# The low part of the squares moves from GpSimd to the Vector engine, with new due times

## The chip, the cores and the metric

The kernel runs on one core of one Trainium2 chip. The metric is the device time of one launch in microseconds (us). Three runs of the kernel before took 1542.89, 1548.58 and 1553.07 us; the median is 1548.58 us.

## The reference

Three layers follow one another on 3072 tokens (4 batches of 768 steps, 8 heads of 40 channels):

```python
for t in range(S):                       # attention with a 40x40 state per batch and head
    y[t] = r[t] @ state
    Sa = state @ a[t]
    state = state * w[t] - outer(Sa, b[t]) + outer(v[t], k[t])
h = x @ w_in                             # first feed-forward: 320 -> 2048 -> 320
g = relu(h) ** 2
x = g @ w_out
p = domain_probs / domain_probs.sum(-1)  # second: 4 experts, 320 -> 1024 -> 320
out = sum(p[:, e] * (relu(x @ w1[e]) @ w2[e]) for e in range(4))
```

All inputs are float32. Where the kernel needs more than one float32r product gives, it splits a number into a rounded high part and a low part (the number minus its high part), and multiplies both.

## The kernel before, in words

**Attention.** The 768 time steps are cut into 12 chunks of 64, and each chunk into two steps by batch pair, so that there are 24 steps s = 0 to 23. Two steps make one block k = 0 to 11. A step loads its inputs (`ld_in`, `ld_r`, `ld_v`, `ld_rf`, `ld_xv`, and the decay factors `ld_wd`), makes running products of the decay with a scan on the Vector engine (DVE; tile `P`, line 379, which reads tile `wd`) and reciprocals of them (line 399), scales k, b and a with them on GpSimd (lines 403 and 411), multiplies them on TensorE (PE), masks results on DVE (lines 493 and 609) and adds the state (lines 624 and 625).

**The inverse.** Each block solves a small triangular system: `invert` reads a matrix `mu` back from DRAM (line 682), runs 31 pairs of DVE instructions on it (line 699 writes `tmp`, line 702 updates `t`, each pair needing the one before), turns the result on ScalarE (ACT, line 709), writes it to DRAM (line 714) and reads it back in another layout (line 723) into `t11` and `TT`. DVE then transposes it (line 564) and PE goes on (line 570). There is one buffer each for `mu` and `t`, so block k + 1 loads `mu` after block k has been written out.

**First feed-forward.** `moe1` takes a block's 256 tokens. SP, the queue that issues the transfers, gathers them with 12 small transfers (line 815); ACT rounds them to `xh` (line 826) and DVE makes the low part `xl` (line 829). Then 16 units follow, one for each 128 hidden channels. A unit has eight products into `h` (line 208, called l1), relu on ACT (`r`, line 761), the square rounded to float32r on ACT (`gh`, line 764), the square in float32 in place (`r`, line 766), the low part `gl = r - gh` (line 769), and six products into `py` (lines 213, 214 and 217, called l2; only line 217 needs `gl`). Its weights come as 48 raw pieces that are decoded during the first blocks.

**Second feed-forward.** After block 10 the attention is over. Block 11 of the first feed-forward and all of the second (lines 971 and on) run in a fixed order with PE as the bound.

**The order of the work.** All engines run their queues in order. For attention, inverse, first feed-forward (blocks 0 to 10) and weight decoding, a planner (class `Schedule`) decides the order once, when the program is built: every operation has an engine, dependences, an assumed duration and a due time, and each engine takes the operation that can start first, and among those the one due first. Due times are a block's start (`DUE["block"]` apart) minus a lead from the table `LEAD`. `PORT` lists operations of DVE and GpSimd that the planner does not let overlap.

Of the kernel before, what the change touches and what calls it, by code (L numbers as in the profile page):

```python
# [7 lines left out]
F32 = mybir.dt.float32  # L8
# [3 lines left out]
ALU = mybir.AluOpType  # L12
# [30 lines left out]
def sub(base, dims):  # L43
# [2 lines left out]

DUE = dict(block=58.06, step=[-2.17, 3.5, -6.04, 5.05, -21.7], invert=[18.92, -23.0, -54.58], ffn=-0.1, w=[-71.6, 2.35])
LEAD = dict(  # L50
    ld_wd=131.3, ld_in=120.8, scan=117.1, m=121.4, t_load=121.1, t=88.2, t_out=173.3, ld_r=73.9, ld_xv=79.2,
    vm=77.6, f=72.9, kbt=67.6, x=65.1, merge=59.0, tx=76.4, ys=65.8, yq=54.5, x1=54.5, split=46.7,
)


class Schedule:
# [11 lines left out]
    STAY = 2.0  # L68

    PORT = dict(  # L70
        DVE=("P", "t", "x1l", "w_clamp", "w_shift", "w_sign", "w_pow", "w_mul"),
        POOL=("sq", "scale_a", "kb", "yq", "yf"),
    )

    def __init__(self):
# [2 lines left out]
    def op(self, name, eng, fn, due, deps=(), dur=0.47, alloc=(), prev=None, lat=None):  # L78
        assert name not in self.ops, name
        lat = (2.1 if eng == "SP" else 0.13) if lat is None else lat  # L80
        self.ops[name] = (eng, fn, due, list(deps) + [prev], dur, alloc, prev, lat)
# [66 lines left out]
def tile_delta_rule_moe(  # L148
# [15 lines left out]
    pe, act, dve, pool, sp = nc.tensor, nc.scalar, nc.vector, nc.gpsimd, nc.sync  # L164
# [55 lines left out]
    op = sch.op  # L220
# [451 lines left out]
    mdd, x1 = {}, {}  # L672
# [84 lines left out]
    def moe1_sq(k, f, i):  # L757
        g = gg[k, f]
        if i == 0:
            g["r"] = fp.tile([128, 256], F32, tag="g0", name=f"r{k}_{f}")  # L760
            act.activation(g["r"], g["ps"], AF.Relu)  # L761
        elif i == 1:
            g["gh"] = fp.tile([128, 256], F32R, tag="gh", name=f"gh{k}_{f}", bufs=3)
            act.activation(g["gh"], g["r"], AF.Square)  # L764
        elif i == 2:
            act.activation(g["r"], g["r"], AF.Square)  # L766
        else:
            g["gl"] = fp.tile([128, 256], F32R, tag="gl", name=f"gl{k}_{f}", bufs=3)
            pool.tensor_tensor(g["gl"], g["r"], g["gh"].bitcast(F32), ALU.subtract)  # L769

    def moe1_l2(k, f):
        if f == 0:
# [15 lines left out]
    def y1_out(k):  # L788
        sp.dma_start(y1d[k], yy[k])
# [15 lines left out]
    def moe1(k, tt):  # L805
        v = {}
        nw = [("w_low", 3 * NF1 - 1)]

        def to_x1(i):
            if i == 0:  # L810
                v["raw"] = buf3(f"xr{k}", "ws", 5).rearrange("p (c x) -> p c x", c=3)
            y = st[2 * k]["y"]
            r0, kc, hd, e0, e1 = MOVES[i]
            src = y[64 * (hd % 2) + e0:64 * (hd % 2) + e1, hd // 2].rearrange("q a x -> q (a x)")
            sp.dma_start(v["raw"][r0:r0 + e1 - e0, kc], src)  # L815

        xt = ("xh", "xl")

        def xbuf(i):
            return ("ws", 5) if k % 2 else (xt[i], 1)  # L820

        def split(i):
            t = buf3(f"{xt[i]}{k}", *xbuf(i))
            t = t.bitcast(F32R).rearrange("p (c x) -> p c x", c=3)
            if i == 0:
                act.copy(t, v["raw"])  # L826
                v["xh"] = t
            else:
                dve.tensor_tensor(t, v["raw"], v["xh"].bitcast(F32), ALU.subtract)  # L829
                x1[k] = (v["xh"], t, v["raw"])  # L830
                if dbg is not None:
                    sp.dma_start(dbg[k], v["raw"])

        ys = [("yq", 2 * k + b, h) for b in range(2) for h in range(2)]
        done = [("x1h", k), ("x1l", k)]
        for i in range(len(MOVES)):
            op(("tx1", k, i), "SP", lambda i=i: to_x1(i), tt - LEAD["x1"], ys + ([] if i else [("x1l", k - 1)]), 0.65, prev=("tx1", k, 0) if i else None,
               alloc=[] if i else [("ws", 5, done)])
        moved = [("tx1", k, i) for i in range(len(MOVES))]
        end = [("l1", k, NF1 - 1)]  # L840
        op(("x1h", k), "ACT", lambda: split(0), tt - LEAD["split"], moved, 0.73, alloc=[xbuf(0) + (end,)])
        op(("x1l", k), "DVE", lambda: split(1), tt - LEAD["split"], [("x1h", k)], 0.87, alloc=[xbuf(1) + (end,)])
        for f in range(NF1):
            t0 = tt + PB * f / NF1
            i = NF1 * k + f
            if i >= units:
                break
            u = lambda d: divmod(i + d, NF1)
            op(("l1", k, f), "PE", lambda f=f: moe1_l1(k, f), t0 - 3,
               [("x1l", k), ("l1",) + u(-1), ("w_low", 3 * f + 2), ("w_low", 3 * f)], 0.9,  # L850
               alloc=[("l1", 2, [("sq", k, f, 0)]), ("g0", 2, [("sq", k, f, 2), ("sq", k, f, 3)])])
            dep = {0: [("l1", k, f)], 3: [("sq", k, f, 2)]}
            al = [None, ("gh", 3, [("l2", k, f)]), None, ("gl", 3, [("l2", k, f)])]
            for j in range(4):
                op(("sq", k, f, j), "POOL" if j == 3 else "ACT", lambda f=f, j=j: moe1_sq(k, f, j), t0 - 2,
                   dep.get(j, [("sq", k, f, j - 1)]) + [("sq",) + u(-1) + (j,)], (0.28, 0.31, 0.31, 0.69)[j],
                   alloc=[al[j]] if al[j] else [])
            op(("l2", k, f), "PE", lambda f=f: moe1_l2(k, f), t0 + 3,
               [("sq", k, f, 3), ("l2",) + u(-1), ("w_low", 3 * f + 1)], 0.85,
               alloc=[("l2", 1, [("y1", k, 0), ("y1", k, 1)])] if f == 0 else [])  # L860
        if NF1 * (k + 1) <= units:
            for t in range(2):
                op(("y1", k, t), "ACT", lambda t=t: y1_copy(k, t), tt + PB - 2, [("l2", k, NF1 - 1)] + ([("y1", k, 0)] if t else []), 0.34,
                   alloc=[] if t else [("ws", 5, [("y1o", k)])])
            op(("y1d", k), "POOL", lambda: y1_double(k), tt + PB + 3, [("y1", k, 0), ("y1", k, 1)], 0.3)
            op(("y1o", k), "SP", lambda: y1_out(k), tt + PB + 4, [("y1d", k)], 0.47)


    nblk = nsteps // 2
    PB, F0 = DUE["block"], 80.0  # L870
    units = NF1 * (nblk - 1)
    for s in range(nsteps):
        attention(s, F0 + PB / 2 * s + DUE["step"][min(s, len(DUE["step"]) - 1)])
    for k in range(nblk):
        invert(k, F0 + PB * k + DUE["invert"][min(k, len(DUE["invert"]) - 1)])
        moe1(k, F0 + PB * k + DUE["ffn"])
    for n in range(3 * NF1):
        weights(n, F0 + DUE["w"][0] + DUE["w"][1] * n)
    sch.run()
    actx.close()  # L880
    items = [divmod(i, NF1) for i in range(units, NF1 * nblk)]
    ffn = []
# [75 lines left out]
    for e, k, f in items:  # L958
# [9 lines left out]
        gh = fp.tile([128, 256], F32R, tag="gh", name=f"zh{e}_{k}_{f}", bufs=3)  # L968
        gl = fp.tile([128, 256], F32R, tag="gl", name=f"zl{e}_{k}_{f}", bufs=3)
# [103 lines left out]
```

## Time and profile before

| | |
|---|---|
| runs | 1542.89, 1548.58, 1553.07 us |
| the profiled execution's own time | 1543.77 us |
| its span, first to last instruction | 1541.9 us |
| mean granted clock of TensorE | 0.977 of full speed |
| busy in the span: PE, DVE, ACT, GpSimd | 1424.5, 810.1, 732.8, 344.7 us |
| 192 instructions of line 769 (`gl`) on GpSimd | 143.9 us, 752 ns each |

The span has three parts: a start until the first block's tokens are split (to 118.9 us), the stretch in which attention and first feed-forward are interleaved (to 799.1 us), and the rest, in which PE hardly pauses. In the rows "idle" is time in which an engine's next instruction waited, with the instruction that released it. POOL is GpSimd in the rows, SPq the queue of transfers, PEclk the granted clock of TensorE.

### The profile page before, as it was taken

How to read it: one execution, taken by the hardware profiler on the slowest of the kernel's cores; microseconds unless marked ns; L12 is line 12 of the kernel's file. 1: busy time of each engine (PE TensorE's matmuls, PEld its weight loads, DVE VectorE, ACT ScalarE, POOL GpSimd, SP SyncE). 2: the span in 40 equal slices, each digit the busy share in tenths (PEclk: the TensorE clock that was granted, in tenths of full speed). 3: DMA queues.
4: the chain of work that ended last, by engine and by line, in shares of the span. 5: the costliest groups of instructions: out<-in, count | busy, mean ns of one | idle time of the engine just before them, and what ended most of it. 6: DMA issues, size and time to landing. Idle time of an engine off the chain costs nothing.

```text
span 1541.9 us, 39676 instructions
## 1 busy us (share of the span) xinstructions
PE 1424.5 (92%) x16336; PEld 1344.1 (87%) x16336; DVE 810.1 (53%) x1992; ACT 732.8 (48%) x1943; POOL 344.7 (22%) x491
## 2 busy tenths in 40 slices
PE   4788989999979888889999999999999999999998
PEld 3567778888878767778889999999999999999998
DVE  6988968769667585766623333223333333233232
ACT  4577767677566565666756333322222222222221
POOL 4223245344343333434234000000000000000000
PEclk9799999999989999999999999999999999999999
DMA  8456344244243441433222112000100100000000
GB/s 245 130 141 171 107 110 119 71 130 134 39 127 79 109 126 41 129 79 81 54 72 86 60 40 77 1 20 20 29 10 1 30 1 1 1 10 27 18 27 27
DMA packets 133908, 107.17 MB, mean 70 GB/s; under 512 B 95968, under 2 KB 108256, under 8 KB 133728
## 3 DMA queue, kind: packets, MB, share of 16 engines
q1 hardware_dynamic: 133728, 104.64, 24.0%
q8 instruction: 129, 2.11, 0.6%
q14 instruction: 51, 0.42, 0.1%
HBM read 85.34 MB, written 14.55 MB: 65 GB/s over the span
## 4 chain that ended last, share of the span: by engine, by line
PE 52%; SPq 1%; DMA 1%; DVE 1%; issue 1%; ACT 1%; POOL 0%; DVEq 0%; ACTq 0%; POOLq 0%
PE z L208 23%; PE pz L214 7%; PE pz L217 7%; PE pz L213 7%; PE h L208 3%; SPq L815 1%; PE py L217 1%; PE py L213 1%; PE py L214 1%; PE ptr L924 1%; DVE xv L609 0%; DMA in<-kba 0%; DMA mu<-md 0%; DMA xr<-y 0%; PE pys L617 0%
## 5 line engine op out<-in xcount | busy, mean ns | idle before, releaser
L971 DVE SCALAR_TENSOR_TENSOR zl<-z,zh 128x256 fp32r<-128x256 f32 x384 | 163.0, 425 | 474.7 <-ACT zh L970 474.7
L970 ACT ACTIVATE zh<-z 128x256 fp32r<-128x256 f32 x384 | 147.1, 383 | 507.1 <-PE z L208 505.4
L208 PE MATMUL z<-x2h,w 128*128 128x256 f32 x1920 | 380.8, 282 | 0.0
L208 PE MATMUL z<-x2l,w 128*128 128x256 f32 x1152 | 320.4, 278 | 0.0
L208 PEld LDWEIGHTS z<-x2h,w 128*128 128x128 f32 x1920 | 306.3, 188 | 0.0
L214 PE MATMUL pz<-w,zh 128*128 128x320 f32 x768 | 231.3, 309 | 0.0
L213 PE MATMUL pz<-w,zh 128*128 128x320 f32 x768 | 230.7, 308 | 0.0
L208 PEld LDWEIGHTS z<-x2l,w 128*128 128x128 f32 x1152 | 216.8, 188 | 0.0
L208 PE MATMUL h<-xh,w 128*128 128x256 f32 x960 | 203.7, 295 | 7.5 <-ACT xh L826 6.8
L769 POOL TENSOR_TENSOR gl<-r,gh 128x256 fp32r<-128x256 f32 x192 | 143.9, 752 | 253.7 <-ACT r L766 157.0
L217 PE MATMUL pz<-w,zl 128*128 128x320 f32 x768 | 175.0, 309 | 0.0
L208 PE MATMUL h<-xl,w 128*128 128x256 f32 x576 | 166.6, 290 | 6.9 <-DVE xl L829 6.7
L208 PEld LDWEIGHTS h<-xh,w 128*128 128x128 f32 x960 | 160.3, 196 | 12.9 <-ACT xh L826 8.6
L699 DVE TENSOR_TENSOR tmp<-mu,t 128x126 f32<-128x126 f32 (+22 forms) x372 | 122.6, 330 | 46.2 <-DMA mu<-md 39.2
L213 PEld LDWEIGHTS pz<-w,zh 128*128 128x128 f32 x768 | 144.4, 188 | 0.0
L214 PEld LDWEIGHTS pz<-w,zh 128*128 128x128 f32 x768 | 144.2, 188 | 0.0
L213 PE MATMUL py<-w,gh 128*128 128x320 f32 x384 | 126.3, 337 | 5.2 <-ACT gh L764 4.9
L196 POOL TENSOR_TENSOR w<-raw,w 64x128 fp32r<-64x128 f32 x32 | 31.9, 996 | 442.9 <-ACT w L194 435.8
L217 PEld LDWEIGHTS pz<-w,zl 128*128 128x128 f32 x768 | 128.4, 188 | 0.0
L761 ACT ACTIVATE r<-h 128x256 f32<-128x256 f32 x192 | 73.3, 382 | 100.6 <-PE h L208 94.9
L208 PEld LDWEIGHTS h<-xl,w 128*128 128x128 f32 x576 | 113.3, 197 | 8.7 <-DVE xl L829 8.7
L214 PE MATMUL py<-w,gh 128*128 128x320 f32 x384 | 118.5, 316 | 0.0
(104 smaller groups left out, 2393.4 us busy)
## 6 DMA issues: line engine op xcount, KB each, us to landing
in<-kba SPq DMA_DIRECT2D x24, 768.0 KB
raw<-wf SPq DMA_DIRECT2D x32, 352.0 KB
raw<-wm SPq DMA_DIRECT2D x32, 234.0 KB
wd<-w SPq DMA_DIRECT2D x24, 264.0 KB
rf<-rv SPq DMA_DIRECT2D x24, 256.0 KB
r<-rv SPq DMA_DIRECT2D x24, 256.0 KB
v<-rv SPq DMA_DIRECT2D x24, 256.0 KB
mu<-md SPq DMA_DIRECT2D x24, 256.0 KB
```

Of the source, the lines that this page charges most:

```text
L196: pool.tensor_tensor(t[64:128, 576:704], raw[64:128, 576:704], t[64:128, 576:704].bitcast(F32), ALU.subtract)
L208: pe.matmul(ps, a, b, start=n == 0, stop=n == len(mm) - 1)
L213: pe.matmul(pys[tt], gh[:, sl], t[:, 256:576], start=first, stop=False)
L214: pe.matmul(pys[tt], gh[:, sl], t[:, 960:1280], start=False, stop=False)
L217: pe.matmul(pys[tt], gl[:, sl], t[:, 256:576], start=False, stop=last)
L699: dve.tensor_tensor(v["tmp"], a, b, ALU.mult)
L761: act.activation(g["r"], g["ps"], AF.Relu)
L769: pool.tensor_tensor(g["gl"], g["r"], g["gh"].bitcast(F32), ALU.subtract)
L815: sp.dma_start(v["raw"][r0:r0 + e1 - e0, kc], src)
L924: pe.transpose(p[:, c], yl[k][:, t, c * 128:c * 128 + 128], ident)
L970: act.activation(gh, ps, AF.Relu)
L971: dve.scalar_tensor_tensor(gl, ps, 0.0, gh.bitcast(F32), ALU.max, ALU.subtract)
```

## The change

`gl` is computed by the same subtraction on DVE instead of GpSimd; the planner is told so (engine DVE, 0.33 us instead of 0.69 us, and the name `sq` moves in `PORT`). The due times and leads are new numbers.

```diff
-DUE = dict(block=58.06, step=[-2.17, 3.5, -6.04, 5.05, -21.7], invert=[18.92, -23.0, -54.58], ffn=-0.1, w=[-71.6, 2.35])
+DUE = dict(block=57.54, step=[-2.27, 3.5, -6.04, 5.05, -24.6], invert=[14.51, -23.23, -54.58], ffn=-0.1, w=[-66.42, 2.42])
 LEAD = dict(
-    ld_wd=131.3, ld_in=120.8, scan=117.1, m=121.4, t_load=121.1, t=88.2, t_out=173.3, ld_r=73.9, ld_xv=79.2,
-    vm=77.6, f=72.9, kbt=67.6, x=65.1, merge=59.0, tx=76.4, ys=65.8, yq=54.5, x1=54.5, split=46.7,
+    ld_wd=141.8, ld_in=118.4, scan=117.1, m=121.1, t_load=116.5, t=92.4, t_out=199.1, ld_r=74.1, ld_xv=81.9,
+    vm=78.1, f=71.6, kbt=67.4, x=63.1, merge=56.7, tx=73.5, ys=65.4, yq=52.7, x1=56.2, split=65.7,
 )
...
-        DVE=("P", "t", "x1l", "w_clamp", "w_shift", "w_sign", "w_pow", "w_mul"),
-        POOL=("sq", "scale_a", "kb", "yq", "yf"),
+        DVE=("P", "t", "x1l", "sq", "w_clamp", "w_shift", "w_sign", "w_pow", "w_mul"),
+        POOL=("scale_a", "kb", "yq", "yf"),
...
-            pool.tensor_tensor(g["gl"], g["r"], g["gh"].bitcast(F32), ALU.subtract)
+            dve.tensor_tensor(g["gl"], g["r"], g["gh"].bitcast(F32), ALU.subtract)
...
-                op(("sq", k, f, j), "POOL" if j == 3 else "ACT", lambda f=f, j=j: moe1_sq(k, f, j), t0 - 2,
-                   dep.get(j, [("sq", k, f, j - 1)]) + [("sq",) + u(-1) + (j,)], (0.28, 0.31, 0.31, 0.69)[j],
+                op(("sq", k, f, j), "DVE" if j == 3 else "ACT", lambda f=f, j=j: moe1_sq(k, f, j), t0 - 2,
+                   dep.get(j, [("sq", k, f, j - 1)]) + [("sq",) + u(-1) + (j,)], (0.28, 0.31, 0.31, 0.33)[j],
```

**Place 1: DVE, the end of one inverse and the start of the next** (block 8 to block 9; in the names the first number is the block or step, for `gl` block and unit). Before:

```order
L699 TENSOR_TENSOR tmp8_30_9580<-mu8_8633,t8_8550 128x16
L702 TENSOR_TENSOR t8_8550<-t8_8550,tmp8_30_9580 128x16
L564 STREAM_TRANSPOSE TT0_89<-t1116_9635 32x8x32 x2
L564 STREAM_TRANSPOSE TT1_90<-t1117_9658 32x8x32 x2
L699 TENSOR_TENSOR tmp9_0_9760<-mu9_9683,t9_9600 128x31
L702 TENSOR_TENSOR t9_9600<-t9_9600,tmp9_0_9760 128x31
L699 TENSOR_TENSOR tmp9_1_9776<-mu9_9683,t9_9600 128x30
L702 TENSOR_TENSOR t9_9600<-t9_9600,tmp9_1_9776 128x30
```

With the change:

```order
L699 TENSOR_TENSOR tmp8_30_9484<-mu8_8553,t8_8455 128x16
L702 TENSOR_TENSOR t8_8455<-t8_8455,tmp8_30_9484 128x16
L769 TENSOR_TENSOR gl7_1_9489<-r7_1_9453,gh7_1_9469 128x256
L769 TENSOR_TENSOR gl7_2_9521<-r7_2_9486,gh7_2_9501 128x256
L769 TENSOR_TENSOR gl7_3_9530<-r7_3_9515,gh7_3_9519 128x256
L769 TENSOR_TENSOR gl7_4_9565<-r7_4_9547,gh7_4_9551 128x256
L769 TENSOR_TENSOR gl7_5_9592<-r7_5_9574,gh7_5_9578 128x256
L564 STREAM_TRANSPOSE TT0_89<-t1116_9549 32x8x32 x2
L769 TENSOR_TENSOR gl7_6_9628<-r7_6_9601,gh7_6_9606 128x256
L564 STREAM_TRANSPOSE TT1_90<-t1117_9576 32x8x32 x2
L769 TENSOR_TENSOR gl7_7_9672<-r7_7_9649,gh7_7_9652 128x256
L699 TENSOR_TENSOR tmp9_0_9683<-mu9_9603,t9_9505 128x31
```

Between the last pair of one inverse (`tmp8_30`) and the first of the next (`tmp9_0`) stood only the two transposes; now seven `gl` of the running feed-forward block stand there, five of them ahead of the first transpose.

**Place 2: SP, after the gather of a block's tokens** (`xr7`; `wd20` are the decay factors of step 20). Before:

```order
L815 DMA xr7_9080<-y14_8850 40x256
L345 DMA rf18_9258<-rv 128x512
L454 DMA md9_9283<-mb18_9212 32x8x32 x4
L341 DMA r18_9310<-rv 128x512
L352 DMA v18_9319<-rv 128x512
L337 DMA wd20_9323<-w 128x528
```

With the change:

```order
L815 DMA xr7_8982<-y14_8761 40x256
L337 DMA wd20_9123<-w 128x528
L345 DMA rf18_9127<-rv 128x512
L454 DMA md9_9226<-mb18_9141 32x8x32 x4
L341 DMA r18_9251<-rv 128x512
L352 DMA v18_9260<-rv 128x512
```

The load of `wd20` moved ahead of the loads of `rf18`, `r18` and `v18` and the four writes of `md9`.

**Place 3: DVE, from the split of a block's tokens (`xl7`) to the scan that reads `wd20`.** Before:

```order
L829 TENSOR_TENSOR xl7_9328<-xr7_9080,xh7_9307 128x768
L702 TENSOR_TENSOR t8_8550<-t8_8550,tmp8_17_9325 128x14x9
L699 TENSOR_TENSOR tmp8_18_9363<-mu8_8633,t8_8550 128x130
L702 TENSOR_TENSOR t8_8550<-t8_8550,tmp8_18_9363 128x13x10
L699 TENSOR_TENSOR tmp8_19_9388<-mu8_8633,t8_8550 128x120
L379 SCALAR_TENSOR_TENSOR P20_9390<-wd20_9323,cs_74 128x264
L702 TENSOR_TENSOR t8_8550<-t8_8550,tmp8_19_9388 128x12x10
L699 TENSOR_TENSOR tmp8_20_9421<-mu8_8633,t8_8550 128x121
L379 SCALAR_TENSOR_TENSOR P20_9390<-wd20_9323,cs_74 128x264
```

With the change:

```order
L829 TENSOR_TENSOR xl7_9228<-xr7_8982,xh7_9164 128x768
L702 TENSOR_TENSOR t8_8455<-t8_8455,tmp8_20_9224 128x11x11
L493 TENSOR_TENSOR xv17_8936<-pv17_0_9188,cs_74 64x4x128 x2
L699 TENSOR_TENSOR tmp8_21_9264<-mu8_8553,t8_8455 128x110
L493 TENSOR_TENSOR xv17_8936<-pv17_1_9189,cs_74 64x4x128
L702 TENSOR_TENSOR t8_8455<-t8_8455,tmp8_21_9264 128x10x11
L493 TENSOR_TENSOR xv17_8936<-pv17_1_9189,cs_74 64x4x128
L699 TENSOR_TENSOR tmp8_22_9301<-mu8_8553,t8_8455 128x108
L769 TENSOR_TENSOR gl6_13_9305<-r6_13_9262,gh6_13_9269 128x256
L702 TENSOR_TENSOR t8_8455<-t8_8455,tmp8_22_9301 128x9x12
L379 SCALAR_TENSOR_TENSOR P20_9327<-wd20_9123,cs_74 128x264
```

Four masking instructions of step 17 (line 493) and one `gl` of the block before (`gl6_13`) now stand between `xl7` and the scan; `xl7` is made while block 6 still has its units 13 to 15 to finish.

## Rows read from the trace of the kernel before

**Rows 1.** Page, part 1: busy time, share of the span, instructions of each engine.
```profile
PE 1424.5 (92%) x16336; PEld 1344.1 (87%) x16336; DVE 810.1 (53%) x1992; ACT 732.8 (48%) x1943; POOL 344.7 (22%) x491
```

**Rows 2.** Windows: stretch, length, busy PE, PEld, DVE, ACT, POOL, granted clock, DMA.
```profile
438.20:505.20 67.00, 57.03 (x888) 50.91 (x888) 43.68 (x105) 41.80 (x113) 25.38 (x38) 0.92 0.37 95
799.10:831.20 32.10, 32.06 (x228) 31.38 (x229) 8.16 (x14) 24.86 (x58) 19.03 (x25) 0.95 0.48 153
831.20:1541.90 710.70, 706.56 (x5444) 706.22 (x5443) 225.59 (x502) 184.69 (x456) 25.05 (x25) 1.00 0.07 23
```

**Rows 3.** Waits of PE, 118.9 to 799.1 us: total, times, longest.
```profile
PE py L217 <- POOL gl L769: 22.4, 19, 2.6
...
PE h L208 <- ACT xh L826: 6.8, 7, 1.6
PE h L208 <- DVE xl L829: 6.1, 7, 1.3
```

**Rows 4.** Waits of DVE in the same stretch.
```profile
DVE P L379 <- DMA wd<-w: 19.9, 5, 6.3
```

**Rows 5.** Windows: one inverse from first to last pair, then until the next.
```profile
602.73:651.65 48.92, 41.31 (x729) 36.56 (x722) 41.99 (x99) 30.57 (x85) 19.72 (x28) 0.93 0.37 106
651.65:667.53 15.88, 14.74 (x173) 13.61 (x174) 1.74 (x6) 10.48 (x27) 5.87 (x10) 1.00 0.33 68
```

**Rows 6.** Timeline of DVE: first instruction of the inverses of blocks 3 and 9.
```profile
281.56 0.48 DVE L699 TENSOR_TENSOR tmp<-mu,t 128x31 f32<-128x31 f32 x1 [4.03 <-DMA mu<-md]
...
667.53 0.21 DVE L699 TENSOR_TENSOR tmp<-mu,t 128x31 f32<-128x31 f32 x1 [4.26 <-DMA mu<-md]
```

**Rows 7.** Page, part 5: the group of the 192 subtractions on GpSimd.
```profile
L769 POOL TENSOR_TENSOR gl<-r,gh 128x256 fp32r<-128x256 f32 x192 | 143.9, 752 | 253.7 <-ACT r L766 157.0
```

**Rows 8.** Timeline of DVE (start, length): a subtraction-sized add and its follower.
```profile
675.30 0.41 DVE L625 TENSOR_TENSOR ys<-pys,FF 128x256 f32<-128x256 f32 x1
675.63 0.26 DVE L699 TENSOR_TENSOR tmp<-mu,t 128x115 f32<-128x115 f32 x1
```

**Rows 9.** Timeline of DVE: two instructions of 45 elements, one after the other.
```profile
649.89 0.21 DVE L699 TENSOR_TENSOR tmp<-mu,t 128x45 f32<-128x45 f32 x1
650.14 0.65 DVE L702 TENSOR_TENSOR t<-t,tmp 128x45 f32<-128x45 f32 x1
```

**Rows 10.** Timeline of GpSimd at the same moment.
```profile
649.99 0.73 POOL L769 TENSOR_TENSOR gl<-r,gh 128x256 fp32r<-128x256 f32 x1 [3.00 <-ACT r L766]
```

**Rows 11.** Windows, instructions on tile gl alone, columns PE, PEld, POOL.
```profile
602.73:651.65 48.92, 5.00 (x19) 3.48 (x20) 6.82 (x9) 0.93 0.37 106
```

**Rows 12.** Timeline of SP right after a gather of tokens.
```profile
565.18 0.42 SPq L345 DMA_DIRECT2D rf<-rv  x1
...
569.39 0.38 SPq L337 DMA_DIRECT2D wd<-w  x1
```

**Rows 13.** Timeline of DVE: the scan that waits for wd.
```profile
575.33 0.71 DVE L379 TENSOR_TENSOR_SCAN P<-wd,cs 128x264 f32<-128x264 f32 x1 [5.56 <-DMA wd<-w]
```

**Rows 14.** Timeline of ACT behind that scan.
```profile
577.19 0.22 ACT L389 COPY g<-P 128x16 f32<-128x16 f32 x1 [3.85 <-DVE P L379]
```

**Rows 15.** Timeline of PE behind that.
```profile
578.19 0.42 PE L213 MATMUL py<-w,gh 128*128 128x320 f32 x1 [2.54 <-ACT gh L764]
```

**Rows 16.** Groups of DVE by line and shape, 0 to 815 us: the masks.
```profile
L493 DVE TENSOR_TENSOR xv<-pv,cs 64x512 f32<-64x512 f32 x96 | 64.3, 686 | 1.7
```

**Rows 17.** Timeline of GpSimd at the start of a block.
```profile
644.27 1.29 POOL L411 TENSOR_TENSOR in<-in,s 128x512 f32<-128x512 f32 x1
645.52 1.47 POOL L769 TENSOR_TENSOR gl<-r,gh 128x256 fp32r<-128x256 f32 x2
```

**Rows 18.** Timeline of PE at that moment.
```profile
646.32 0.56 PE L217 MATMUL py<-w,gl 128*128 128x320 f32 x2 [2.63 <-POOL gl L769]
```

**Rows 19.** Timeline of ACT: the turn of the inverse that ended at 651.65 us.
```profile
653.86 1.07 ACT L709 COPY mu<-t 128x512 f32<-128x512 f32 x1
```

**Rows 20.** Waits of GpSimd, 118.9 to 799.1 us.
```profile
POOL gl L769 <- ACT r L766: 151.5, 79, 8.6
```

## The prediction, made before the run

> **What bounds the kernel now.** I read the page first: PE is busy for 92% of the span [rows 1]. That is an average over two different parts, so I cut the span with the view of windows. From 831.2 us on PE is busy for 706.56 of 710.70 us, and in the block before that for 32.06 of 32.10 us [rows 2]. Nothing that takes load from another engine can shorten this part. What the change can move lies between 118.9 and 799.1 us. A block there looks like the first row of the group: 67.00 us, PE busy for 57.03, at a granted clock of 0.92 [rows 2].
>
> Next I asked what PE waits for in that stretch. The longest entry is the product of line 217 waiting for `gl` from GpSimd, 22.4 us in 19 waits; the first products of a block wait another 6.8 and 6.1 us for `xh` and `xl` [rows 3]. That is an upper bound for what goes when these waits go, not what the stretch gets shorter by, so I looked for a loop that repeats once per block. There is one on DVE. From the first to the last pair of an inverse 48.92 us pass, in which DVE is busy for 41.99; until the next inverse another 15.88 us pass, in which it is busy for 1.74, because the result has to be turned, written to DRAM, read back, and only then does the next matrix come in [rows 5]. The inverses of blocks 3 and 9 begin at 281.56 and 667.53 us [rows 6]: six rounds in 385.97 us, 64.3 us each, which is also the length of a block. **So I take the period of a block to be this loop**: some 49 us in which DVE works almost without pause, then 16 us of transfers. What lengthens or shortens DVE's 49 us moves the end; what lies in the 16 us does not.
>
> **The change part by part.** The sum is made over these six rounds and against the profiled execution's own 1543.77 us, which is 4.8 us below the median of 1548.58.
>
> *gl leaves GpSimd.* There it costs 752 ns each [rows 7]. GpSimd is not the bound, so its time counts only through who waits for it. The order of the changed kernel has all 192 on DVE, so the change does what it says.
>
> *gl arrives on DVE.* The nearest row is an add of the same 128x256 floats, 0.41 us long; its follower starts 0.33 us after it [rows 8]. In place 1 of the orders seven `gl` of a round stand where DVE idles for its 16 us; those cost nothing as long as the transfers there stay as late as now. If they came earlier, seven times 0.33 us would show. The other `gl` of the six rounds lie inside the 49 us. I counted 66 in the order: 66 x 0.33 = **+22 us**, with 66 x 0.41 = +27 as the upper end and 0, if they fill the small holes of DVE, as the lower one.
>
> The Trainium skill (VectorE: DVE Perf Modes, "The DRAIN you can't avoid") says that the next DVE instruction starts only when the pipeline has emptied. By that rule each `gl` would cost its full 0.41 us and the forecast would be 5 us higher. The row with its overlap of 0.08 us speaks for the smaller price in this mix.
>
> *What GpSimd's gl did to DVE.* Two instructions of 45 elements stand side by side: the first takes 0.21 us, the second 0.65, and the second runs while GpSimd has a `gl` from 649.99 to 650.72 [rows 9, 10]. So one `gl` on GpSimd can cost DVE 0.44 us. Nine of them lie in the 49 us of a round [rows 11]. All nine colliding would give back 9 x 0.44 x 6 = 24 us, none of them 0. I take six of nine: near the upper end, since DVE is busy for 41.99 of the 48.92 us [rows 5], but below it, since a `gl` may also fall on a hole: 6 x 0.44 x 6 = **-16 us**.
>
> The Trainium skill (SBUF — State Buffer, "Who interferes with whom") says that a DVE instruction with two SBUF inputs and a GpSimd instruction that reads SBUF exclude each other and the later one blocks fully. The rows agree: the held instruction ended 0.07 us after the `gl`. By the rule as far as it goes, a whole 0.73 us for each of nine, the gain would be 39 us instead of 16, near the time of the first rival below. The rule also speaks against the change, for `gl` on DVE has two SBUF inputs and can now be held by GpSimd's scaling itself; GpSimd's scaling holds DVE in either kernel, though, and only the instruction held differs.
>
> *The load of wd moves.* Place 2 of the orders puts it ahead of seven other issues. One round shows what its lateness does: `rf` is issued at 565.18 us, `wd` only at 569.39 [rows 12]; the scan waits for it for 5.56 us [rows 13], ACT behind the scan 3.85 us [rows 14], PE behind ACT 2.54 us [rows 15]. With the change `wd` is issued where `rf` was, 4.2 us earlier, and place 3 puts four masks of 686 ns [rows 16] in front of the scan, another 2.7 us. Together 6.9 us, more than the longest of the five waits, 6.3 us. All five, 19.9 us in sum [rows 4], should go: **-20 us** (ends: 0 and -20). The seven issues that `wd` passes come one issue, 0.38 us, later; they serve a product and a matrix needed later, and no wait of PE for them stands among the long ones.
>
> *The turn.* The inverse that ends at 651.65 us is turned by ACT from 653.86 on [rows 19], 2.2 us late, since ACT first serves feed-forward units that PE's waits have delayed. With fewer such waits I take 1 us per round, **-6 us** (ends 0 and -13).
>
> *PE's waits for gl* need no entry of their own: they end where the loop lets them. Their worst case is at a block's start, where `gl` stands on GpSimd behind scaling of 1.29 us and PE stops for 2.63 us [rows 17, 18]. On DVE that queue is gone. Nor does the start of the kernel get an entry (two pieces of weights fewer stand before the first block, and more of the attention in block 0; 6 us either way), and in the last block the 16 `gl` find DVE busy for 8.16 of 32.10 us while PE is full [rows 2]: nothing.
>
> Sum: +22 - 16 - 20 - 6 = **-20 us**, 1523.8 us in a profiled execution, and **1529 us** against the median. With the ends of the terms it goes from -41 to +11 around that, which I narrow, since the ends do not come together, to 1517 to 1545 us.
>
> **The rivals.** *1. PE's waits were the bound, and all of them go.* For it: 22.4 + 6.8 + 6.1 = 35.3 us of waits [rows 3], and a clock of 0.92 in a block of 67.00 us, 5 us of lost work [rows 2], which full speed gives back in part. The split of the tokens moves to where five PE steps of work remain, so the 12.9 us at block starts should go too. Against it: DVE has no room for so much shorter a period. Price: -35 - 5 = -40 us, 1508 us. Chance 0.17.
>
> *2. DVE becomes tighter and eats the gain.* The collisions stay, with `gl` the one that is held, and each `gl` costs 0.41 us. For it: DVE is already busy for 41.99 of 48.92 us [rows 5]. Against it: GpSimd has 144 us less to do. Price: +27 - 20 = +7 us, 1556 us. Chance 0.23.
>
> *3. Slower: DVE waits for ACT at each gl.* On GpSimd `gl` waited for ACT's square for 151.5 us in 79 waits, 1.9 us each, and it cost nobody anything [rows 20]. On DVE the pairs of the inverse, the masks and the additions to the state stand behind a waiting `gl`, and PE waits for those. For it: the planner assumes 0.31 us for a square and cannot know how late it is. Against it: inside the 49 us DVE is the later engine, ACT busy for only 30.57 [rows 5], so the square should be there first. Price: 66 `gl` at w us each; w = 0.3 eats the forecast's 20 us, w = 0.54 makes the kernel slower by 1%. At a third of the 1.9 us it is 66 x 0.63 = 42, in sum +22 us, 1570 us. Chance 0.12.
>
> **How the numbers follow.** A measurement of this kernel tells 1%, 15.5 us, from no change: faster is below 1533, slower above 1564. The forecast has 0.48, and its own range lies for two thirds below 1533: 0.31 faster, 0.17 same. Rival 1 adds 0.17 faster, rival 2 adds 0.23 same, rival 3 adds 0.09 slower and 0.03 same. Faster 0.48, same 0.43, slower 0.09. The range from 1508 to 1556 takes in both nearer rivals and leaves out rival 3 and the tails.
>
> **What would show it.** Right: rounds from `tmp` to `tmp` of some 61 us instead of 64.3; no wait of the scan for `wd`; `gl` at some 0.4 us on DVE; fewer pair instructions of 0.6 us and more; no wait of PE for `gl` behind GpSimd's scaling. Wrong: waits of DVE on ACT's square at line 769, a window of the inverse that stays at 49 us, waits of the scan that remain, or a period that falls well below 61 us, which would make PE's waits the bound and not DVE.

## The result, and the profile after

| | kernel before | changed kernel |
|---|---|---|
| median, same chip | 1550.39 us | 1531.34 us |
| profiled execution / its span | 1543.77 / 1541.9 us | 1529.88 / 1528.1 us |
| ratio, 95% interval | | 0.9909 (0.9881 to 0.9938) |

The change is worth 0.9%, some 14 us (19.05 us between the medians of four runs each, 13.9 between the two profiled executions). The forecast was 1529 us, 1.3% faster. By the prediction's bound of 1% the ratio lies just inside "same", and its interval reaches to both sides of that bound.

The page of the changed kernel, part 1 and the group of `gl` (they answer to [rows 1] and [rows 7]):

```profile
PE 1417.1 (93%) x16336; PEld 1339.8 (88%) x16336; DVE 864.1 (57%) x2184; ACT 732.4 (48%) x1943; POOL 212.9 (14%) x299
...
L769 DVE TENSOR_TENSOR gl<-r,gh 128x256 fp32r<-128x256 f32 x192 | 88.2, 460 | 100.5 <-ACT r L766 97.8
```

DVE has 88.2 us of `gl` more, but only 54.0 us more busy time. Of the 34.2 us between them, 17.8 are `gl` that run beside other instructions of DVE (one begins before the one in front has ended), and 16.4 are that those 1992 other instructions cover less time: 793.7 us instead of 810.1.

The six rounds of the prediction, first `tmp` of each end (answering to [rows 6]). One label has to be put right first: these are the inverses of blocks 4 and 10, not 3 and 9.

```profile
278.38 0.21 DVE L699 TENSOR_TENSOR tmp<-mu,t 128x31 f32<-128x31 f32 x1 [4.18 <-DMA mu<-md]
...
642.74 0.21 DVE L699 TENSOR_TENSOR tmp<-mu,t 128x31 f32<-128x31 f32 x1 [1.55 <-DMA mu<-md]
```

They now take 364.36 us instead of 385.97, 60.7 each; some 61 was forecast. The view of windows over the six rounds, of before and then of after (length, busy PE, PEld, DVE, ACT, POOL, granted clock, DMA share, GB/s):

```profile
281.56:667.53 385.97, 339.06 (x5388) 305.59 (x5383) 267.80 (x619) 252.08 (x676) 157.16 (x234) 0.96 0.36 97
```

```profile
278.38:642.74 364.36, 327.82 (x5361) 294.18 (x5356) 291.34 (x718) 248.84 (x668) 88.68 (x132) 0.99 0.38 103
...
582.37:628.89 46.52, 40.45 (x713) 35.86 (x708) 44.96 (x109) 31.31 (x87) 14.95 (x19) 0.96 0.36 103
628.89:642.74 13.85, 13.85 (x187) 13.17 (x189) 4.44 (x12) 9.74 (x25) 0.78 (x3) 1.00 0.47 107
```

PE idles 36.5 us of the rounds instead of 46.9. The last two rows answer to [rows 5]: the stretch from the first to the last pair fell from 48.92 to 46.52 us although DVE is busy for 2.97 us more in it. Summed over the six stretches, DVE's idle time fell from 35.2 to 13.8 us and its busy time rose by 6.7.

The waits in the rounds (total, times, longest): DVE before, DVE after, PE before, PE after.

```profile
DVE TT L564 <- DMA t<-td: 57.6, 12, 9.2
DVE tmp L699 <- DMA mu<-md: 28.9, 7, 4.3
DVE P L379 <- DMA wd<-w: 17.1, 4, 6.3
```

```profile
DVE gl L769 <- ACT r L766: 42.3, 35, 2.2
DVE tmp L699 <- DMA mu<-md: 18.3, 7, 4.2
```

```profile
PE py L217 <- POOL gl L769: 18.9, 14, 2.6
```

```profile
PE py L217 <- DVE gl L769: 6.4, 10, 1.4
```

The scan's wait for `wd` is gone. DVE does wait for ACT's square, as the third rival said, but nearly all of it (all but 2.7 us of the 42.3) falls into the gap of the transfers, where it used to wait for `t` anyway.

So the rounds gained 21.6 us and the kernel 13.8. The place where it was given back shows on PE, when it first uses the inverse of block 4 and of block 10 (line 570). Before:

```profile
337.35 0.69 PE L570 MATMUL py<-TT,m 32*32 32x32 f32 x32
...
718.15 0.69 PE L570 MATMUL py<-TT,m 32*32 32x32 f32 x32
```

After:

```profile
334.48 0.24 PE L570 MATMUL py<-TT,m 32*32 32x32 f32 x2
...
694.81 0.22 PE L570 MATMUL py<-TT,m 32*32 32x32 f32 x2 [0.19 <-DMA TT<-td]
```

Up to the first point 2.9 us are won, between the two 20.5, but from 718.15 on the kernel before needed 823.8 us more and from 694.81 on the changed one 833.3: 9.5 us are lost. In the written order PE has 152 feed-forward units behind it at that second point before and 148 now. Sixteen units took 32.10 us where PE is full [rows 2], 2.0 each, so four units are 8 us of the 9.5. Behind that point PE is in fact busy for 820.7 us instead of 812.7. The units were not saved, only moved behind the rounds. Counted from the first `tmp` of each end, as in the table below, 3.2 us are won ahead of the rounds, 21.6 in them, and 11.0 are lost behind them.

### The profile page after: what moved, and what is told of

Its sections match the earlier page's. It is cut to its first block, busy times and chain, and to the rows that moved or that the text cites. A ratio compares the mean times of both kernels' runs of the same rounds, so it can differ in the third digit from the quotient of the medians.

```text
span 1528.1 us, 39610 instructions
## 1 busy us (share of the span) xinstructions
PE 1417.1 (93%) x16336; PEld 1339.8 (88%) x16336; DVE 864.1 (57%) x2184; ACT 732.4 (48%) x1943; POOL 212.9 (14%) x299
## 4 chain that ended last, share of the span: by engine, by line
PE 59%; DVE 18%; DMA 8%; SPq 5%; ACT 4%; issue 4%; POOL 1%; DVEq 0%; POOLq 0%; ACTq 0%
PE z L208 24%; PE pz L214 7%; PE pz L217 7%; PE pz L213 7%; PE h L208 4%; DVE tmp L699 3%; DVE t L702 3%; DVE xv L493 3%; SPq L815 3%; DVE xv L609 2%; DMA mu<-md 2%; DMA td<-mu 2%; DVE gl L769 1%; SPq L723 1%; PE py L217 1%
## 5 line engine op out<-in xcount | busy, mean ns | idle before, releaser
L208 PE MATMUL h<-xh,w 128*128 128x256 f32 x960 | 198.6, 290 | 3.5 <-ACT xh L826 3.3
L769 DVE TENSOR_TENSOR gl<-r,gh 128x256 fp32r<-128x256 f32 x192 | 88.2, 460 | 100.5 <-ACT r L766 97.8
L699 DVE TENSOR_TENSOR tmp<-mu,t 128x126 f32<-128x126 f32 (+22 forms) x372 | 113.3, 305 | 30.0 <-DMA mu<-md 24.6
L702 DVE TENSOR_TENSOR t<-t,tmp 128x126 f32<-128x126 f32 (+22 forms) x372 | 115.7, 311 | 6.0
```

Source lines behind the costliest of these rows:

```text
L208: pe.matmul(ps, a, b, start=n == 0, stop=n == len(mm) - 1)
L699: dve.tensor_tensor(v["tmp"], a, b, ALU.mult)
L702: dve.tensor_tensor(c, c, v["tmp"], ALU.subtract)
L769: dve.tensor_tensor(g["gl"], g["r"], g["gh"].bitcast(F32), ALU.subtract)
```

## The experiments

Eleven kernels ran. Each ratio is to the kernel before on the same chip, with its 95% interval; 0.001 is 1.5 us. The other columns are sums over the six rounds of the profiled execution: their length from the first `tmp` of block 4 to that of block 10; the part of it from first to last pair; DVE's idle time in that part; and how long after DVE's last pair ACT begins the turn (line 709). "Rest" is the time from block 10's first `tmp` to the end.

| run | ratio | rounds | first to last pair | DVE idle there | turn late | rest |
|---|---|---|---|---|---|---|
| before | 1 | 386.0 | 292.6 | 35.2 | 11.4 | 874.4 |
| e1 gl on DVE, old order | 1.0006 (0.9980 to 1.0033) | 387.0 | 302.2 | 28.6 | 2.3 | 877.4 |
| e3 wd early | 1.0014 (0.9990 to 1.0038) | 386.6 | 281.2 | 25.5 | 23.8 | 874.5 |
| e9 turn early | 1.0003 (0.9975 to 1.0030) | 386.1 | 305.9 | 53.8 | 0.2 | 882.5 |
| e10 turn and wd early | 0.9945 (0.9920 to 0.9971) | 375.9 | 285.8 | 30.6 | 10.1 | 883.4 |
| e11 gl on DVE, wd early | 0.9954 (0.9926 to 0.9981) | 377.8 | 293.1 | 27.3 | 2.5 | 875.6 |
| e6 new times, gl on GpSimd | 1.0013 (0.9978 to 1.0049) | 384.7 | 288.3 | 21.5 | 14.7 | 878.4 |
| e2 new order, gl on GpSimd | 0.9964 (0.9940 to 0.9987) | 370.0 | 280.6 | 13.2 | 4.5 | 887.4 |
| e5 gl on DVE, old times | 0.9958 (0.9928 to 0.9988) | 363.5 | 275.2 | 14.5 | 0.8 | 886.8 |
| changed kernel | 0.9909 (0.9881 to 0.9938) | 364.4 | 277.9 | 13.8 | 0.6 | 885.4 |
| e4 changed, wd late | 0.9921 (0.9884 to 0.9958) | 366.9 | 281.1 | 16.2 | 1.1 | 886.4 |
| e8 changed, prob late | 0.9912 (0.9878 to 0.9947) | 368.0 | 282.3 | 16.5 | 0.6 | 884.9 |
| e7 changed, gl twice | 1.0192 (1.0157 to 1.0226) | 394.0 | 307.0 | 13.6 | 1.3 | 894.8 |

These columns come from one execution each. e8 runs the changed kernel's program up to the last block, and yet its rounds are 3.6 us longer and begin 1.7 us later; differences of that size in the columns say nothing.

### First four: the parts alone

**e1**, the engine alone, in the old order:

```diff
-            pool.tensor_tensor(g["gl"], g["r"], g["gh"].bitcast(F32), ALU.subtract)
+            dve.tensor_tensor(g["gl"], g["r"], g["gh"].bitcast(F32), ALU.subtract)
```

> The kernel before with one edit: the low part of the squares (gl) is written by DVE, at the very place in the order where GpSimd wrote it; every other instruction and transfer stays where it was. Theory A (the block period is a loop on DVE: its 49 us from the first pair of the inverse to the last, and the transfers after it; what the change won came mostly from the earlier load of wd): some 60 to 72 gl's of about 0.33 us come onto DVE inside the six rounds (+20 to +24 us), some 6 us of them are bought back as collisions of GpSimd's gl with DVE go (up to 16), the waits for wd stay: the time stays within -5 and +15 us of the kernel before. Theory B (the end is set by PE's waits for gl on GpSimd, 22.4 us, and the engine move alone takes them away): -12 to -20 us.

Measured: nothing, as theory A said. The first-to-last stretches grew by 9.6 us and the turn came 9.1 us less late.

**e2**, the reverse edit in the changed kernel (`dve` to `pool` in that line):

> The changed kernel with one edit: gl goes back to GpSimd; the order of everything else, the early load of wd included, stays that of the changed kernel. Theory A: the waits of DVE's scan for wd stay away (17 us of the six rounds), DVE has 60 gl's less, but gl stands behind the scaling of a on GpSimd and PE waits for it as before or longer: -8 to -14 us against the kernel before. Theory B: the waits of PE for gl come back (22 us or more), so the time is that of the kernel before, within 4 us.

Measured: -0.36%, 5.6 us: between the two theories, a little nearer to B's ±4 than to A's -8. The wait of PE for `gl` did not come back: 7.8 us in the rounds on GpSimd, 6.4 on DVE, 18.9 in the kernel before. So here the order took PE's waits for `gl` away and the engine was not needed for it. It is not the only way: in the old order they are 16.6 us with `gl` on DVE (e1) and 7.5 with `wd` loaded early as well (e11 below). What the engine gives in the new order is read from the page of e2:

```profile
PE 1416.2 (92%) x16336; PEld 1336.5 (87%) x16336; DVE 832.9 (54%) x1992; ACT 732.5 (48%) x1943; POOL 352.6 (23%) x491
```

DVE without a single `gl` is busy for 832.9 us; in the changed kernel the same 1992 instructions cover 793.7. GpSimd's 192 `gl` cost DVE's other work 39.2 us there, against 19.0 in the old order (810.1 before, 791.1 in e1).

**e3**, the load of `wd` alone:

```diff
...
+        for s in range(6, NSTEP, 2):
+            at = {x[3]: i for i, x in enumerate(q)}
+            i, j = at["ld_wd", s], at["ld_rf", s - 2]
+            if at["P", s - 1, 1] < j < i:
+                q.insert(j, q.pop(i))
...
```

(`q` is the finished order; the item moves on SP's queue only. `...` stands for lines left out: the function around the loop and its call.)

> The kernel before with one edit: on SP's queue the load of wd for the next-but-one step stands ahead of the loads of rf, md, r and v of the step in front of it, as in the changed kernel; every engine's own order is that of the kernel before. Theory A: the waits of DVE's P for wd (19.9 us, 17 of them in the six rounds) go from the loop, so -12 to -17 us against the kernel before. Theory B: DVE catches up at its next wait and nothing reaches the end: within 3 us of the kernel before.

Measured: nothing. Theory A fails here. Its waits did go, and the stretches became 11.4 us shorter; but the turn came 12.4 us later. Of these, 9.9 us fall into the last of the six rounds (12.1 us late instead of 2.2); the other five together became 2.4 us shorter, the last 3.1 longer. The last round shows it. The timelines of DVE, ACT and PE in e3 (start, length, in brackets the wait):

```profile
644.92 0.18 DVE L702 TENSOR_TENSOR t<-t,tmp 128x16 f32<-128x16 f32 x1
...
649.04 0.90 PE L217 MATMUL py<-w,gl 128*128 128x320 f32 x2 [6.63 <-POOL gl L769]
...
651.74 0.38 ACT L761 ACTIVATE r<-h 128x256 f32<-128x256 f32 x1 [8.54 <-PE h L208]
...
657.23 1.08 ACT L709 COPY mu<-t 128x512 f32<-128x512 f32 x1
```

The last pair ends at 645.10. The turn stands in ACT's order behind the activations of units that PE has not multiplied yet, and PE in turn waits 6.63 us for a `gl` of GpSimd. ACT comes to the turn 12.1 us after DVE is done. In that round DVE's gain became a wait in ACT's queue.

**e4**, the reverse in the changed kernel:

```diff
...
+        for s in range(6, NSTEP, 2):
+            at = {x[3]: i for i, x in enumerate(q)}
+            i, j = at["ld_wd", s], at["ld_v", s - 2]
+            if i < j < at["P", s, 0]:
+                q.insert(j, q.pop(i))
...
```

> The changed kernel with one edit: on SP's queue the load of wd goes back behind the loads of rf, md, r and v of the step in front of it; gl stays on DVE and every engine's order is that of the changed kernel. Theory A: DVE's P waits for wd again, some 3 us in a round: +10 to +17 us over the changed kernel, about 1543, close to the kernel before. Theory B: the changed kernel's time within 3 us, 1528 to 1534.

Measured: the changed kernel's time within the error. But this run doesn't price the wait, since it hardly came back: 0.9 us in the six rounds. The place of the load is not what took the wait away in the changed kernel; which of the other moved steps did is open.

### The parts of the diff: e5 to e8

**e5** is the changed kernel with `DUE` and the two lines of `LEAD` put back to their old numbers. Against the kernel before it changes the engine of `gl` and what the planner knows of it (engine, 0.33 us, `PORT`).

> The changed kernel with one edit: the due times and leads are those of the kernel before; gl is on DVE and the planner knows it (0.33 us, one port for DVE and GpSimd). What the first four runs left: DVE's scan no longer waiting for wd is worth nothing (e3, e4), the engine of gl alone nothing (e1), the order alone 4 to 6 us (e2), both 12 to 19. Theory C (what counts is the order that the refitted due times give: PE's six rounds from the inverse of block 4 to that of block 10 last 386 us in every kernel with the old times and 364 to 370 in every one with the new): the rounds stay at 380 us or more and the time within 4 us of the kernel before. Rival D (what counts is that the planner places gl rightly on DVE; the new times are only a consequence): -8 us or more against the kernel before.

**e6** is the opposite: the kernel before with only these three lines taken from the changed one.

> The kernel before with one edit: the due times and leads are those of the changed kernel; gl stays on GpSimd and the planner knows it (0.69 us). Theory C: the rounds shorten to some 370 us, but GpSimd's gl's lie beside DVE's work (in e2 they lengthen DVE's other instructions by 89 us between 118 and 800 us against 65 before), so the time is that of e2, -3 to -8 us against the kernel before. Rival D: the new times fit gl on DVE alone, and with gl on GpSimd they give nothing or a loss: 0 to +8 us.

Measured: e5 -0.42% with rounds of 363.5 us, e6 nothing with rounds of 384.7. Theory C had the two the wrong way round, on rounds as on times; rival D was nearer, though its -8 us or more for e5 came to -6.5. The rounds become short because the planner knows that `gl` is on DVE and takes 0.33 us there, and places all engines' work by that; the same engine at the old place (e1) leaves them at 387.0. (The 89 and 65 us in the expectation of e6 are not the price of `gl` alone: by the swaps e2 and e1 that is 39.2 and 19.0 us.) What the new numbers add to e5 is 7.5 us between the profiled spans (1535.6 and 1528.1), and 7.0 of it lie ahead of the rounds: block 4's inverse begins at 285.4 us in e5, at 278.4 in the changed kernel (at 277.0 in e4 and 280.1 in e8, so 2 to 3 us of it can be chance).

**e7** doubles the suspected cost:

```diff
-            dve.tensor_tensor(g["gl"], g["r"], g["gh"].bitcast(F32), ALU.subtract)
+            for _ in range(2): dve.tensor_tensor(g["gl"], g["r"], g["gh"].bitcast(F32), ALU.subtract)
```

> The changed kernel with one edit: DVE writes each gl twice, the same values (192 instructions more, by the rows of the changed kernel 0.36 to 0.46 us each, 70 to 88 us of DVE). Theory A as predicted (the six rounds are a loop in which DVE is nearly always busy from the inverse's first pair to its last): the 60 gl's inside those stretches add 22 us to the rounds, so +15 to +30 us over the changed kernel. Theory C (PE's work and PE's waits set the end, DVE's time counts where PE has run out of work ahead): PE's last matmuls of a unit get gl some 0.36 us later where they wait at all (15 of 192 in the changed kernel), and DVE catches up in the gap at the transfers: +2 to +10 us.

Measured: 1577.76 us, some 44 to 47 us above the changed kernel, more than either theory said and far from C's 2 to 10. The six rounds took 29.6 us more (A: 22 for the `gl` inside them); of the 47.2 us between the profiled spans another 8.1 lie ahead of the rounds and 9.5 behind them. Windows of e7 over the rounds, then the waits of DVE and of PE in them:

```profile
286.50:680.46 393.96, 341.28 (x5323) 303.50 (x5316) 337.38 (x816) 249.08 (x666) 91.47 (x132) 0.95 0.36 95
```

```profile
DVE gl L769 <- ACT r L766: 32.9, 32, 2.8
```

```profile
PE py L217 <- DVE gl L769: 22.5, 21, 2.6
```

Inside the stretches DVE's busy time rose by 29.3 us, its idle time stayed at 13.6 (10.9 of that are holes under 0.15 us between instructions), and the turn is still only 1.3 us late. In the changed kernel, time added on DVE therefore passes into the rounds nearly one to one, while in the kernel before stretches shorter by 11.4 us (e3) gave nothing. Two things stay open: e7 also makes PE wait 16.1 us longer for `gl`, and no run shortened DVE's work in the changed kernel, so what that would give back is not shown.

**e8** takes the stall out of the last block: the four instructions of the probabilities (lines 902 to 905) go behind the loop over the feed-forward units.

> The changed kernel with one edit: in the last block the four DVE instructions of the probabilities stand behind the feed-forward units' gl's instead of in front of them, so no gl is queued behind the reduce that waits 5.9 us for the transfer of prob. If that wait was given back at the end: -3 to -6 us against the changed kernel, and PE's 3.3 us wait at py for gl at 786 us gone. Rival: PE then waits at the next thing that the last block brings late (the weights, or xs of the last block), and the time is the changed kernel's within 2 us.

The stall in the changed kernel, on DVE and on PE:

```profile
787.83 0.25 DVE L902 TENSOR_REDUCE psum__13043<-prob 128x24 f32<-128x96 f32 x1 [5.93 <-DMA prob<-dp]
...
789.32 0.56 PE L217 MATMUL py<-w,gl 128*128 128x320 f32 x2 [3.33 <-DVE gl L769]
```

Measured: the same time. In e8 the longest wait of PE for a `gl` in that stretch is 1.4 us, but another takes its place, at 798 us:

```profile
798.09 0.47 PE L208 MATMUL h<-xh,w 128*128 128x256 f32 x1 [2.33 <-ACT r L761]
```

So that this stall was 3 to 6 us of what was given back is not confirmed; with four runs the interval is 5 us to either side.

### The last three: two paces

What e1 to e8 left is theory E: a round has two paces, DVE's and that of PE with ACT behind it, and the later one counts.

**e9**, the kernel before with ACT's turn six activations earlier from block 4 on (only ACT's own order differs):

```diff
...
+        for k in range(4, NBLK):
+            at = {x[3]: i for i, x in enumerate(q)}
+            i = at["tt", k]
+            a = [j for j in range(i) if self.ops[q[j][3]][0] == "ACT"][-6]
+            up = [x for x in q[a:i] if x[3][:2] == ("t", k)] + [q[i]]
+            q[a:i + 1] = up + [x for x in q[a:i] if x not in up]
...
```

> The kernel before with one edit: from the inverse of block 4 on, ACT's copy that turns the finished inverse for its way out (L709) stands two units (six activations) earlier on ACT; every other engine's order, SP's queue included, is that of the kernel before. Theory E (two paces: DVE's, from the inverse's first pair to its last; and that of PE with ACT behind it, whose place in the order decides when the turn comes. In the kernel before DVE is done some 2 us before ACT comes to the turn, 11.4 us in six rounds, since ACT's activations ahead of it wait for PE's h; in the changed kernel 0.6): the lag goes to about 1 us in six rounds and the time falls by 5 to 12 us. Rival F (PE's own work and waits set the round, and an inverse that comes sooner only waits for PE): within 3 us of the kernel before.

Measured: nothing, as rival F said; E's 5 to 12 us did not come. The turn is late by 0.2 us in sum and the gaps shrank by 13.2 us, yet the stretches grew by 13.3. DVE's waits in e9's rounds:

```profile
DVE P L379 <- DMA wd<-w: 18.3, 4, 5.7
DVE xv L609 <- PE ptx L605: 12.3, 6, 3.0
DVE xl L829 <- ACT xh L826: 7.0, 5, 2.4
```

An inverse that starts earlier finds `wd` as late as ever, and DVE now waits 12.3 us for products of PE, 0.2 before.

**e10** and **e11** join two edits that gave nothing alone: e3 with e9, and e1 with e3.

> The kernel of e3 (wd early) with the same one edit as e9 (ACT's turn two units earlier). Theory E: in e3 DVE's waits for wd went and the lag before ACT's turn rose from 11.4 to 23.8 us in six rounds, which is why it gained nothing; with the turn earlier the lag falls to 5 us or less and both gains show: -12 to -22 us against the kernel before. Rival F: within 3 us of the kernel before, as e3.

> The kernel of e1 (gl on DVE at GpSimd's place in the order) with wd loaded early on SP as in e3; nothing else moved. Theory E: in e1 the lag before ACT's turn is 2.3 us in six rounds, so DVE sets the pace there, and the 11.7 us that its scans wait for wd inside those rounds come off: -7 to -14 us against e1 and the kernel before. Rival F: DVE's time is not what is waited for, as in e3: within 3 us of the kernel before.

Measured: -0.55% and -0.46%, 8.5 and 7.1 us, where F said no change. Three edits at no gain each (e1, e3, e9) make two pairs with a gain. E is right in that; its size for e10 was too large (-12 to -22). PE's waits for GpSimd's `gl` stay there (23.1 us in the rounds, 18.9 before) and the turn is still 10.1 us late; that these are the reason is not shown. Nor does the trace of e10 show where its gain lies: the profiled execution was the slowest of its ten, 1545.25 us against a median of 1539.18, and loses behind the rounds 9.0 of the 10.1 us won in them. Windows of both rounds, e10 first:

```profile
284.19:660.07 375.88, 332.65 (x5320) 303.25 (x5316) 265.62 (x618) 250.46 (x668) 155.54 (x232) 0.95 0.37 100
```

```profile
280.47:658.27 377.80, 334.25 (x5422) 300.47 (x5422) 288.56 (x720) 253.70 (x678) 86.44 (x132) 0.99 0.37 99
```

Neither reaches the changed kernel. In e11, 11.2 us of DVE's idle time inside the stretches are `gl` waiting for ACT's square; in the changed kernel 2.7. Those are 8.5 of the 13.5 us by which DVE idles less in the changed kernel's stretches than in e11's. No version here beats the changed kernel.

The view of the critical chain (the chain of work that ended last, followed back from the end) tells the two kinds of kernel apart. Its shares of the six rounds, the changed kernel first, then e1 and e11 (the view ends each line where it is cut here):

```profile
by line: DVE t L702 8.0%; DVE tmp L699 7.9%; DMA mu<-md 7.0%; issue 6.8%; DVE xv L493 6.5%; DVE xv L609 6.3%; SPq L815 5.8%; DMA td<-mu 5.6%; SPq L723 4.6%; PE h L208 4.3%; DVE gl L769 4.1%; DMA in<-kba 3.7%; DVE q L399 2.6%; PE pys L617 1.
```

```profile
by line: PE h L208 9.5%; DMA wd<-w 5.4%; DVE gl L769 5.4%; DVE xv L609 5.2%; SPq L815 4.8%; issue 4.7%; DMA mu<-md 4.5%; DVE xv L493 4.2%; DVE tmp L699 4.1%; DVE t L702 3.6%; PE py L217 3.6%; PE pys L617 2.6%; DMA td<-mu 2.5%; DVE q L399 2.
```

```profile
by line: PE h L208 12.8%; issue 9.1%; DMA in<-kba 7.8%; DMA mu<-md 6.9%; DVE gl L769 4.8%; DVE tmp L699 4.0%; DVE t L702 4.0%; PE py L217 4.0%; DVE xv L609 3.5%; PE py L213 3.3%; SPq L815 3.1%; PE pys L617 2.8%; PE py L214 2.7%; DMA xr<-y 2
```

Summed by engine, the chain in the changed kernel's rounds is 41% DVE and 15% PE; in the old order it is mixed, 31% DVE and 27% PE in e1, 23% and 32% in e11, 24% and 30% in e9. In the kernel before the chain reaches back only to 646.3 us, so that it says nothing of those rounds.

## Why the prediction was right, and where it was not

**The sum over the rounds was right: -20 forecast, -21.6 measured.** Its ends were not: those of the four terms add up to -57 and +27, not to -41 and +11; the measured time lies inside the stated range all the same. The parts, as the traces show them:

| term | forecast | measured in the rounds |
|---|---|---|
| `gl` on DVE, first to last pair | 66 x 0.33 = +22 | 63: +18.8 (alone on DVE) to +25 (start to start) |
| collisions gone | -16 | -12.0 to -18 |
| waits for `wd` | -20 | -17.1 |
| turn of the inverse | -6 | -10.8 (11.4 to 0.6) |

- *gl on DVE* and *collisions*: the net, +6.7 against +6, was right, and the trace divides it no more sharply than the table. The 63 `gl` are 28.5 us long, 0.45 each, but overlap their neighbours; they have DVE to themselves for 18.8 us, and the same 594 other instructions cover 12.0 us less (245.3 instead of 257.4). The overlap shows here:

```profile
280.07 0.42 DVE L769 TENSOR_TENSOR gl<-r,gh 128x256 fp32r<-128x256 f32 x1
280.40 0.21 DVE L702 TENSOR_TENSOR t<-t,tmp 128x56 f32<-128x56 f32 x1
```

The follower starts 0.33 us after the `gl`, as in [rows 8]; where it came without a wait of over 0.15 us (122 of the 192), the median is 0.34 and the mean 0.39, which makes 25 us for the 63. The rule of the Trainium skill that I set aside (VectorE: DVE Perf Modes, "The DRAIN you can't avoid": the next instruction starts only when the pipeline has emptied, though the same section says that one that is not held starts earlier) would give 0.41; here 118 of the 192 followers start before their `gl` has ended.
- *Collisions.* GpSimd's `gl` did hold DVE's instructions, by 19.0 us in the old order and 39.2 in the new one over the whole kernel, 0.10 and 0.20 us per `gl`: the size depends on what lies beside them. And a `gl` on DVE can be held in its turn, as the prediction feared; in the changed kernel one that starts beside GpSimd's scaling takes 1.51 us:

```profile
319.42 1.27 POOL L411 TENSOR_TENSOR in<-in,s 128x512 f32<-128x512 f32 x1
...
319.46 1.51 DVE L769 TENSOR_TENSOR gl<-r,gh 128x256 fp32r<-128x256 f32 x1
```

The Trainium skill (SBUF — State Buffer, "Who interferes with whom": a DVE instruction with two SBUF inputs contends with a GpSimd instruction that reads SBUF) says as much, and the trace agrees in both directions.
- *wd.* **Here a step failed: "What lengthens or shortens DVE's 49 us moves the end."** In the kernel before it does not: e3 shortened these stretches by 11.4 us and the rounds by nothing, because ACT then came to the turn 12.4 us later, 9.9 of that in one round. The load alone is worth 0, beside another edit 7 to 8.5 us (e10, e11), and in the changed kernel its place is not what keeps the wait away (e4). I added up terms that cannot be added: e1, e3 and e9 gave nothing one by one and something in pairs. For time added, the sentence is true of the changed kernel (e7).
- *The turn* was seen and its cause named (ACT behind units that PE's waits delay), but as a small extra of 6 us. It was the sign of the second pace. It also goes against the prediction's own "what lies in the 16 us does not" move the end: the turn lies there, and 10.8 us of the rounds' gain with it.
- *"Nothing" for the start and the last block* is the other step that failed. From line 570 on 9.5 us were given back after the rounds, 8 of them four feed-forward units that the new order leaves for later. That could have been counted in the order: units ahead of line 570, 152 against 148. Counted from the first `tmp`, the start gave 3.2 us (some 7 against e5, which has the old numbers) and the rest took 11.0: so -21.6 became -13.8.

**The rivals.** The first (PE's waits all go, 1508 us) had part of the mechanism: PE's waits for `gl` in the rounds fell from 18.9 to 6.4 us, and the granted clock of the rounds rose from 0.96 to 0.99. PE's idle time in the whole kernel fell by only 6.4 us, since other waits grew. Its 5 us for the clock counted one block; PE's busy time in the six rounds fell by 11.2. The second (`gl` dear, collisions stay, 1556) was wrong on the collisions; its 0.41 us for a `gl` is just above the 0.30 (alone on DVE) to 0.39 (start to start) that one took. The third (DVE waits for the square, 1570) is not at work in the changed kernel, 2.7 us, though e11 shows the wait where the planner had not placed `gl`.

So the time was right for a reason that is half right, and by some luck: of what the rounds won, the parts put at nothing took back 7.8 us. The loop on DVE is the bound *after* the change (e7 and the chain). That before it DVE and PE with ACT waited for each other in turns is argued from e1, e3, e9, e10 and e11 and not seen directly.

## What to carry to other kernels

When two chains of engines hand work to each other every round, a wait that you see on one of them may be worth nothing by itself; you need to know when the other is ready: look for the first instruction after the loop's end and for how late its engine comes to it. Cost a new order over a whole period, counting the work that it leaves for later (here four units of PE), and not only the loop. And tell the planner the engine and the price of a moved step: the same move was worth nothing at its old place and 6.5 us where the planner had placed it (the runs do not separate engine from price).

## What the runs showed of the hardware

- The 192 subtractions on GpSimd lengthened DVE's other work by 19.0 us in one order and 39.2 in another: here contention depended on the schedule, not on the instruction alone.
- On DVE the same instruction averaged 460 ns on the page, and its follower began 0.34 us after it (median). A second copy of each, into the same tile, began 0.45 us after the first (median) and added 85.8 us to DVE's busy time (949.9 - 864.1), 0.45 us each.
- PE's busy time, not only its idle time, depends on the order: 1424.5 to 1427.4 us in the kernels before, e1, e3 and e6, 1416.2 to 1419.2 in the changed one, e2, e4 and e8, with the same 16336 products. In the rounds of the first the granted clock was 0.95 to 0.97, a mean of its levels of 2.4 and 1.2 GHz, in those of the second 0.98 to 0.99, where PE stood idle less (46.8 to 49.3 us and 36.5 to 42.3). Idle time alone does not decide it: in e10 and e11 PE stood idle for 43.2 and 43.5 us of the rounds, at 0.95 and 0.99.
